# Attention in one table of steps per pair of heads, with one ring of seven PSUM banks

## The chip, the cores and the metric

One core of a Trainium2 chip. TensorE (PE) multiplies and transposes into PSUM (8 banks); ScalarE (ACT), VectorE (DVE) and GpSimd (POOL) work on tiles; SyncE (SP) issues the DMAs from one queue, in order. The metric is the device time of one execution in microseconds (us).

## The reference

Three stages on 896 tokens (2 batches of 448), 12 heads of 64:

```python
# 1: causal attention, q, k, v of shape (2, 12, 448, 64)
scores = np.where(mask, -1e9, (1 / np.sqrt(64)) * (q @ k.T))
attn = np.exp(scores - max); attn = attn / (sum + 1e-9)
x = (attn @ v) as (896, 768)
# 2: h = x @ w_in (768 x 2048); g = 0 below -1, h above 1, (h + 1)**2 / 4 between; x = g @ w_out
# 3: xn = x / rms(x) * rms_g; g = xn @ w_gate; x = (silu(g) * (xn @ w_val)) @ w_out  (768 x 1536)
```

## The kernel before

The program is recorded as a list of operations (`Plan.op`), each with the engines it may run on and a planned length. `Plan.run` puts them in time by their dependences and emits them per engine in the order of the planned starts. Operations recorded through `seq` keep their recorded order on their engine (a chain); the others fill the places between them.

The attention works on pairs of heads: 12 pairs g, each with three units of score chunks: unit 0 is row chunk 3 (448 columns), unit 1 row chunks 2 and 0 (336 and 112 columns), unit 2 row chunk 1 (224 columns). In this document the steps have short names, a digit for the unit and a second one for the head j:

- S (`scores`, L763): the scores of both heads of a unit into two PSUM banks.
- M (`maxima`, L771, DVE): adds the mask and takes the row maximum, in place in the bank.
- E (`exps`, L780, ACT): exponential out of the bank into SBUF (`pn`), with the row sum; after it the bank is free.
- T (`transposes`, L799): TensorE transposes the exponentials into one or two banks. V (`evac`, L823 on ACT, L825 on DVE): copies them to SBUF (`pts`); of the five copies of a pair one is on DVE.
- PV (`pv`, L852): the product with the values into bank 7.
- F (`factor`, L831, L833 on DVE): reciprocals of the sums, then DMAs on SP to DRAM (L835) and back as a broadcast `rb` (L838, two halves).
- X (`xsplit`, L862, DVE): multiplies PV's bank by `rb` into x; after it `operand` makes the operands of the next stage (a cast and a subtraction for each, L298 and L304, often a subtraction ahead).

S takes banks from a ring of four (`sring`), T from a ring of three (`tring`), each in fixed turns; PV has bank 7. The loop over n = 3 g + u records scores(n + 1), maxima(n), exponentials(n), transposes(n - 1), the copies of unit n - 2, and PV of pair g - 1 at u = 2. q is multiplied by 1/8 after it is loaded (`scale_q`, L743: pair 0 on DVE, the others on POOL).

Between these steps the weights of in1 (`w_in`) are loaded and prepared: `w_float` (L346 on ACT, L349 and L359 on DVE) makes fp32 of 64-bit words in blocks of 128 x 768, `split` makes a rounded part (`copy_op`, a cast on ACT, L298) and a remainder (`tt_op`, DVE or POOL, L304). Four such blocks are prepared by the end of the attention.

The next stage, in1 (L491), is made of units of 9 matmuls of 448 columns, one unit for each product of a group of weights (seven products per group; the first unit is product 1 of group 0). It starts once the last PV is through. Then come `plain` (L1026), the second matrix pair (L491 again) and `outer` (L561).

Of the kernel before, what the change touches and what calls it, by code (L numbers as in the profile page):

```python
# [10 lines left out]
F32 = mybir.dt.float32  # L11
# [207 lines left out]
def kernel(  # L219
# [65 lines left out]

    def bank_take():
        i = min(bfree, key=lambda i: bfree[i])
        del bfree[i]
        return i
# [7 lines left out]
    def copy_op(dst, src, n, r, w, **kw):  # L297
        op({"ACT": act_t(n)}, lambda e: nc.scalar.copy(dst, src), r, w, **kw)  # L298
# [29 lines left out]
    def w_float(st, ps, wf):  # L328
# [11 lines left out]
        def words(w, dtype):  # L340
            return ap(st, dtype).rearrange("p (n t) -> p n t", t=2)[:, :, w]

        top = ("top", st.off, len(plan.alts))
        low = ("low", st.off, len(plan.alts))
        op({"ACT": act_t(n)},
           lambda e: nc.scalar.activation(words(1, F32), words(1, F32), ACTF.Prelu, scale=2.0 ** -112,  # L346
                                          alpha=-2.0 ** 32), [st], [top])
        op({"DVE": (dve2_t(n), True)},
           lambda e: nc.vector.tensor_scalar(out=words(0, I32), in0=words(0, I32), scalar1=29, scalar2=0,  # L349
                                             op0=ALU.logical_shift_right, op1=ALU.bitwise_or), [st], [low])  # L350

        def comb(e):
            out, hi, lo = words(1, I32), words(1, I32), words(0, I32)
            if ps:
                out = pst[:, 6:8, :HW].bitcast(I32)
                hi, lo = (x.rearrange("p (h n) -> p h n", h=2) for x in (hi, lo))
            else:
                out = ap(wf, I32)
            nc.vector.scalar_tensor_tensor(out=out, in0=hi, scalar=3, in1=lo, op0=ALU.logical_shift_left,  # L359
                                           op1=ALU.bitwise_or)  # L360
        op({"DVE": (dve_t(n), True)}, comb, [top, low], [st] + ([bk(6), bk(7)] if ps else [wf]))
# [342 lines left out]
    mask = SF.alloc(S)  # L704
    held = qraw + kraw + vraw + [pn] + pts + rbs + [mask]
# [630 lines left out]
```

## Time and profile before

| | us |
|---|---|
| runs: median of 3 (lowest to highest) | 573.09 (568.79 to 574.65) |
| the profiled execution | 571.67 |
| its span | 570.0 |

| engine | busy us | share of the span |
|---|---|---|
| PE | 552.1 | 97% |
| DVE | 476.5 | 84% |
| ACT | 377.5 | 66% |
| POOL | 89.5 | 16% |

The first 102.8 us are the attention, then follows in1 until 206.3. A busy share is an average over stages, and a matmul that has begun and waits inside its group still counts as busy; so the rows below follow the chain of work that ended last and the timeline of single rounds.

### The profile page before, as it was taken

Reading aid. Unit: us, or ns where it says so; the run is one execution under the profiler, and the core shown is the slowest. Engines: PE = TensorE matmul, PEld = TensorE weight load, DVE = VectorE, ACT = ScalarE, POOL = GpSimd, SP = SyncE. Lnnn points to the kernel's source line nnn. Section 1 sums busy time; section 2 is a strip of 40 time slices with the busy share of each in tenths; the row PEclk is TensorE's granted clock in tenths of the full one; section 3 lists DMA queues with packets and bytes.
Section 4 is the critical chain, followed back from the end, with each engine's and each line's share of the span. In section 5 each row is a group of like instructions: output and inputs, shape, how many; then the busy total and the mean of one; then the engine's idle time right before and its main releaser. Section 6 shows DMA issues by size and latency. Waiting matters only on the chain.

```text
span 570.0 us, 8284 instructions
## 1 busy us (share of the span) xinstructions
PE 552.1 (97%) x2890; PEld 475.1 (83%) x2890; DVE 476.5 (84%) x932; ACT 377.5 (66%) x807; POOL 89.5 (16%) x86
## 2 busy tenths in 40 slices
PE   6999998999999999999999988999999999999997
PEld 4555655899998899998999877999989999999896
DVE  4898667999989889844983599999899998999993
ACT  5899888768877888636542553377565748756751
POOL 2323143101002010000000111253301010101400
PEclk9999999999999999999999978999999999999999
DMA  8644633142145468413030310163542434341012
GB/s 257 180 142 137 179 98 67 59 164 99 67 167 160 145 209 281 149 55 110 3 112 0 112 54 0 53 227 111 173 160 112 135 142 163 120 162 48 1 48 97
DMA packets 21496, 67.80 MB, mean 119 GB/s; under 512 B 5264, under 2 KB 11408, under 8 KB 21456
## 3 DMA queue, kind: packets, MB, share of 16 engines
q1 hardware_dynamic: 21456, 67.30, 35.9%
q8 instruction: 22, 0.36, 0.3%
q14 instruction: 18, 0.15, 0.1%
HBM read 64.49 MB, written 2.80 MB: 118 GB/s over the span
## 4 chain that ended last, share of the span: by engine, by line
PE 86%; DVE 6%; DMA 3%; ACT 3%; issue 1%; POOL 0%; SPq 0%; DVEq 0%; ACTq 0%
PE ps L491 38%; PE ps L1026 20%; PE ps L561 13%; PE ps L763 7%; PE ps L799 4%; PE ps L852 4%; DVE sf L304 2%; DMA sf<-in_w_in 1%; DVE sr L304 1%; DMA sf<-in_w_gate 1%; ACT sr L298 1%; DVE sf L359 1%; DVE sf L349 1%; DMA sf<-in_qT 0%; DVE ps L359 0%
## 5 line engine op out<-in xcount | busy, mean ns | idle before, releaser
L491 PE MATMUL ps<-sr 128*128 128x448 f32 x1260 | 262.2, 370 | 1.8 <-ACT sr L298 1.1
L491 PEld LDWEIGHTS ps<-sr 128*128 128x128 f32 x1260 | 239.0, 190 | 24.7 <-ACT sr L298 1.9
L298 ACT CAST sr<-sf 128x384 fp32r<-128x384 f32 (+2 forms) x260 | 137.4, 557 | 81.7 <-DVE sf L304 28.0
L304 DVE TENSOR_TENSOR sr<-sf,sr 128x448 fp32r<-128x448 f32 (+2 forms) x218 | 131.5, 628 | 23.4 <-ACT sr L298 19.0
L1026 PE MATMUL ps<-sr 128*128 128x448 f32 x576 | 118.6, 367 | 0.0
L1026 PEld LDWEIGHTS ps<-sr 128*128 128x128 f32 x576 | 108.2, 188 | 10.1 <-issue 0.4
L304 POOL TENSOR_TENSOR sr<-sf,sr 128x384 fp32r<-128x384 f32 (+2 forms) x42 | 53.0, 1267 | 304.8 <-ACT sr L298 298.0
L304 DVE TENSOR_TENSOR sf<-ps,sf 128x448 f32<-128x448 f32 (+1 forms) x113 | 66.4, 597 | 14.5 <-PE ps L491 7.8
L561 PE MATMUL ps<-sr 128*128 128x448 f32 x378 | 77.1, 366 | 0.0
L561 PEld LDWEIGHTS ps<-sr 128*128 128x128 f32 x378 | 70.8, 188 | 6.2 <-ACT ps L298 0.4
L304 DVE TENSOR_TENSOR sf<-sf 128x448 f32<-128x448 f32 (+1 forms) x88 | 56.0, 663 | 19.0 <-ACT sf L964 18.7
L346 ACT ACTIVATE sf<-sf 128x768 f32<-128x768 f32 x68 | 62.0, 922 | 8.0 <-DMA sf<-in_w_in 2.4
L771 DVE CUSTOM_DVE_ANT_0 ps<-ps,sf 112x336 f32<-112x336 f32 (+2 forms) x96 | 41.8, 465 | 17.5 <-PE ps L763 16.5
L780 ACT ACTIVATE sf<-ps,sf 112x336 f32<-112x336 f32 (+2 forms) x96 | 47.3, 509 | 6.9 <-DVE sf L771 6.0
L359 DVE SCALAR_TENSOR_TENSOR sf<-sf 128x768 int32<-128x768 int32 x50 | 48.3, 975 | 1.4 <-ACT sf L346 0.4
L763 PE MATMUL ps<-sf 64*112 64x448 f32 (+3 forms) x192 | 42.5, 447 | 6.9 <-DVE sf L743 4.5
L304 POOL TENSOR_TENSOR sf<-sf 128x448 f32<-128x448 f32 (+1 forms) x24 | 29.2, 1226 | 88.1 <-DVE sf L304 52.5
L349 DVE TENSOR_SCALAR sf<-sf 128x768 int32<-128x768 int32 x68 | 41.0, 609 | 2.3 <-DMA sf<-in_w_in 0.9
L298 ACT CAST sr<-ps 128x384 fp32r<-128x384 f32 (+1 forms) x54 | 25.4, 489 | 20.0 <-DVE ps L304 8.3
L763 PEld LDWEIGHTS ps<-sf 64*112 64x112 f32 x192 | 18.3, 180 | 22.4 <-ACT sf L780 6.7
L304 DVE TENSOR_TENSOR sr<-ps,sr 128x384 fp32r<-128x384 f32 (+1 forms) x54 | 30.1, 560 | 3.9 <-ACT sr L298 3.1
L298 ACT COPY ps<-ps 128x448 f32<-128x448 f32 x36 | 18.7, 521 | 18.3 <-PE ps L491 17.0
(45 smaller groups left out, 346.2 us busy)
## 6 DMA issues: line engine op xcount, KB each, us to landing
sf<-in_w_out SPq DMA_DIRECT2D x28, 768.0 KB, 4.3
sf<-in_w_in SPq DMA_DIRECT2D x16, 768.0 KB, 4.3
sf<-in_w_gate SPq DMA_DIRECT2D x12, 768.0 KB, 4.3
sf<-in_w_val SPq DMA_DIRECT2D x12, 768.0 KB, 4.5
sf<-in_kT SPq DMA_DIRECT2D x12, 224.0 KB, 3.2
sf<-in_qT SPq DMA_DIRECT2D x12, 224.0 KB, 4.4
sf<-in_v SPq DMA_DIRECT2D x12, 224.0 KB, 3.3
sf<-row SPq DMA_DIRECT2D x24, 112.0 KB, 2.9
```

The lines of the kernel that those rows point to most:

```text
L298: op({"ACT": act_t(n)}, lambda e: nc.scalar.copy(dst, src), r, w, **kw)
L304: op(alts, lambda e: E[e].tensor_tensor(out=dst, in0=a, in1=b, op=alu), r, w, **kw)
L346: lambda e: nc.scalar.activation(words(1, F32), words(1, F32), ACTF.Prelu, scale=2.0 ** -112, alpha=-2.0 ** 32), [st], [top])
L349: lambda e: nc.vector.tensor_scalar(out=words(0, I32), in0=words(0, I32), scalar1=29, scalar2=0, op0=ALU.logical_shift_right, op1=ALU.bitw ...
L359: nc.vector.scalar_tensor_tensor(out=out, in0=hi, scalar=3, in1=lo, op0=ALU.logical_shift_left, op1=ALU.bitwise_or)
L491: nc.tensor.matmul(bank(o), lhsT=ap(d.sub(x * HW + k * P, P)), rhs=ap(t.sub(y * S, S)), start=(begin and k == 0 and i == 0), stop=(k == HK ...
L561: nc.tensor.matmul(bank(o), lhsT=ap(a.sub(x * HW + d * P, P)), rhs=ap(t.sub(y * S, S)), start=(p == 1 and i0 == 0 and i == 0), stop=(i0 == ...
L763: nc.tensor.matmul(pst[:C, bs[j], o:o + (c + 1) * C], lhsT=ap(q)[r, c * C:(c + 1) * C], rhs=ap(k)[r, :(c + 1) * C], start=True, stop=True, ...
L771: seq("DVE", 0.19 + 0.00105 * (c + 1) * C + 0.14, lambda t=t, c=c: nc.vector.tensor_tensor_reduce(out=t, in0=t, in1=ap(mask)[:C, S - (c + ...
L780: seq("ACT", 0.2 + 0.0008 * w + 0.2, lambda c=c, o=o, w=w: nc.scalar.activation(Pn[:C, j, poff[c]:poff[c] + w], pst[:C, sbank[n][j], o:o + ...
L799: nc.tensor.transpose(pst[:C, bs[j][0], o:o + C], Pn[:C, j, poff[c] + kc * C:poff[c] + (kc + 1) * C], ap(ident)[:C, :C])
L1026: nc.tensor.matmul(bank(o), lhsT=ap(w.sub(x * NK * P + d * P, P)), rhs=ap(t.sub(y * S, S)), start=(i0 == 0 and i == 0), stop=(i0 == NM - 1 ...
```

## The change

- **Order.** The loop over n is replaced by a table, `PIPE`, that is walked once per pair: each entry is a step, its unit, its head or half, and a shift of the pair (0, -1 or -2). The recorded order of TensorE's work in a round is S0(g), PV(g-2), T2(g-1), T1(g-1), S2(g), S1(g), T0(g). ACT's is E10, E11, V01, V00 of pair g-1, E01 of g, V20 of g-1, E00 of g, V11 of g-1, E20, E21 of g; V10 is DVE's.
- **Banks.** One ring of seven for S and T: a step takes the bank that was given back the longest ago (`bank_take`), and E or V gives it back. PV keeps bank 7. Bank 6 is reserved from pair NG on.
- **1/8.** `scale_q` is gone; the maximum multiplies by -1/8 instead of -1.
- **Operand casts.** While `early` holds (until the walk reaches pair NG), a cast from SBUF may go to POOL, and `w_float` works in two halves of 384 columns.
- **in1's first unit** is recorded between the last T and the last PV (`run_unit`).
- Ten tiles for x are set aside (`xslots`), and some planned lengths are changed.

TensorE's instructions for one round in the middle of the attention, before (112x448: S0; 64x...: PV; 112x112: T; 112x336, 112x112 x2 and 112x224 of L763: S1 and S2):

```order
L763 MATMUL ps<-sf 112x448 x2
L852 MATMUL ps<-sf 64x336 x2
L852 MATMUL ps<-sf 64x112 x2
L852 MATMUL ps<-sf 64x336 x2
L852 MATMUL ps<-sf 64x224 x2
L852 MATMUL ps<-sf 64x112 x2
L799 MATMUL ps<-sf 112x112 x8
L763 MATMUL ps<-sf 112x336 x2
L763 MATMUL ps<-sf 112x112 x2
L799 MATMUL ps<-sf 112x112 x4
L763 MATMUL ps<-sf 112x224 x2
L799 MATMUL ps<-sf 112x112 x8
```

and of the change:

```order
L765 MATMUL ps<-sf 112x448 x2
L856 MATMUL ps<-sf 64x336 x2
L856 MATMUL ps<-sf 64x112 x2
L856 MATMUL ps<-sf 64x336 x2
L856 MATMUL ps<-sf 64x224 x2
L856 MATMUL ps<-sf 64x112 x2
L802 MATMUL ps<-sf 112x112 x12
L765 MATMUL ps<-sf 112x224 x2
L765 MATMUL ps<-sf 112x336 x2
L765 MATMUL ps<-sf 112x112 x2
L802 MATMUL ps<-sf 112x112 x8
```

The instructions are the same; T1 has moved from the end of the round to behind PV, next to T2, and stands for the pair before, and S1 stands last among the scores.

TensorE from the last PV but one to in1, before (L491: in1):

```order
L852 MATMUL ps<-sf 64x112 x2
L799 MATMUL ps<-sf 112x112 x12
L852 MATMUL ps<-sf 64x336 x2
L852 MATMUL ps<-sf 64x112 x2
L852 MATMUL ps<-sf 64x336 x2
L852 MATMUL ps<-sf 64x224 x2
L852 MATMUL ps<-sf 64x112 x2
L491 MATMUL ps<-sr 128x448 x504
```

and of the change (L504: in1):

```order
L856 MATMUL ps<-sf 64x112 x2
L802 MATMUL ps<-sf 112x112 x12
L504 MATMUL ps<-sr 128x448 x9
L856 MATMUL ps<-sf 64x336 x2
L856 MATMUL ps<-sf 64x112 x2
L856 MATMUL ps<-sf 64x336 x2
L856 MATMUL ps<-sf 64x224 x2
L856 MATMUL ps<-sf 64x112 x2
L504 MATMUL ps<-sr 128x448 x495
```

Nine of in1's matmuls, its first unit, now stand ahead of the last PV.

POOL in the later half of the attention, before (L743: the scaling of q; L304: subtractions and additions):

```order
L743 TENSOR_SCALAR sf<-sf 128x448
L304 TENSOR_TENSOR sr<-sf,sr 128x448
L304 TENSOR_TENSOR sr<-sf,sr 128x384
L743 TENSOR_SCALAR sf<-sf 128x448
L304 TENSOR_TENSOR sr<-sf,sr 128x448
L743 TENSOR_SCALAR sf<-sf 128x448
L304 TENSOR_TENSOR sr<-sf,sr 128x448
L304 TENSOR_TENSOR sf<-sf 128x448
```

and of the change (L305: casts; L311: subtractions and additions):

```order
L305 CAST sr<-sf 128x448
L311 TENSOR_TENSOR sr<-sf,sr 128x448
L311 TENSOR_TENSOR sf<-sf 128x384
L305 CAST sr<-sf 128x384
L311 TENSOR_TENSOR sf<-sf 128x448
L305 CAST sr<-sf 128x448
L311 TENSOR_TENSOR sr<-sf,sr 128x448
L305 CAST sr<-sf 128x384
```

The scalings are gone, and the casts that were ACT's have come.

The diff, cut to its core:

```diff
+    reserved = set()
     def bank_take():
-        i = min(bfree, key=lambda i: bfree[i])
+        i = min((i for i in bfree if i not in reserved), key=lambda i: bfree[i])
...
-    def copy_op(dst, src, n, r, w, **kw):
-        op({"ACT": act_t(n)}, lambda e: nc.scalar.copy(dst, src), r, w, **kw)
+    early = [True]
+    def copy_op(dst, src, n, r, w, ps=True, **kw):
+        alts = {"ACT": act_t(n)}
+        if not ps and early[0]:
+            alts["POOL"] = pool_t(n)
+        op(alts, lambda e: nc.scalar.copy(dst, src) if e == "ACT" else nc.gpsimd.tensor_copy(dst, src), r, w, **kw)
...
+        parts = 2 if early[0] and not ps else 1
+        m = n // parts
+        for i in range(parts):
...
+    xslots = [SF.alloc(S) for _ in range(10)]
...
-    def scale_q(g, eng):
-        if g < NG:
-            q = qraw[g % NQ]
-            seq(eng, 0.6, lambda: E[eng].tensor_scalar(out=ap(q), in0=ap(q), scalar1=float(D) ** -0.5, scalar2=1.0,
-                                                       op0=ALU.mult, op1=ALU.mult), [q], [q])
-    sring, tring = [0, 1, 2, 3], [4, 5, 6]
-    def turn(ring):
-        ring.append(ring.pop(0))
-        return ring[-1]
...
-        sbank[n] = bs = [turn(sring), turn(sring)]
+        sbank[n] = bs = [bank_take(), bank_take()]
...
-                out=t, in0=t, in1=ap(mask)[:C, S - (c + 1) * C:], scale=-1.0, scalar=3e38,
+                out=t, in0=t, in1=ap(mask)[:C, S - (c + 1) * C:], scale=-float(D) ** -0.5, scalar=3e38,
...
+        bank_give(sbank[n][j])
...
-            tbank[n] = [(turn(tring), 0), (turn(tring), 0)]
+            tbank[n] = [(bank_take(), 0), (bank_take(), 0)]
...
+        bank_give(t)
...
+    PIPE = (
+        ("S", 0, 0), ("M", 1, 1, -1), ("E", 1, 0, -1), ("PV", -2), ("E", 1, 1, -1), ("M", 0, 1, 0), ("V", 0, 1, -1),
...
+    VEC = {(1, 0)}
...
+    bfree.pop(7)
...
+    for g in range(NG + 2):
+        if g == NG:
+            reserved.add(6)
+            early[0] = False
+        for what in PIPE:
+            if 0 <= g + what[-1] < NG:
+                if g == NG + 1 and what[0] == "PV":
+                    run_unit()
+                step(what[:-1], g + what[-1])
+        if g < NG:
+            emit_preps(min(2 * g - 16, -3), -1)
```

## Rows read from the trace of the kernel before

**Rows 1.** Windows: stretch; us, then each engine's busy us; TensorE clock, DMA share, GB/s.

```profile
23.98:87.12 63.14, 61.71 (x448) 36.75 (x448) 49.65 (x173) 56.02 (x181) 22.01 (x25) 1.00 0.52 146
...
102.81:206.30 103.49, 103.34 (x507) 94.59 (x506) 94.61 (x163) 82.47 (x154) 14.79 (x11) 1.00 0.38 128
```

**Rows 2.** Chain that ended last, 38 to 50 us: start, us, engine and line.

```profile
40.08 1.82 PE ps L763 x4
41.90 2.04 PE ps L852 x20
43.94 0.91 PE ps L799 x8
44.85 0.95 PE ps L763 x8
45.79 0.53 PE ps L799 x4
46.32 0.57 PE ps L763 x4
46.89 0.91 PE ps L799 x8
```

**Rows 3.** Timeline, same round: start, us, engine, line, operation; [idle before <-releaser].

```profile
40.89 0.27 PEld L763 LDWEIGHTS ps<-sf 64*112 64x112 f32 x2 [0.57 <-ACT sf L780]
...
45.83 0.52 DVE L771 CUSTOM_DVE_ANT_0 ps<-ps,sf 112x336 f32<-112x336 f32 x1 [0.24 <-PE ps L763]
...
46.87 0.54 ACT L780 ACTIVATE sf<-ps,sf 112x336 f32<-112x336 f32 x1
...
47.47 0.95 DVE L862 TENSOR_TENSOR sf<-ps,sf 128x448 f32<-128x448 f32 x1
...
47.73 0.54 ACT L780 ACTIVATE sf<-ps,sf 112x336 f32<-112x336 f32 x1
```

**Rows 4.** Chain that ended last, 0 to 25 us.

```profile
4.02 0.41 DVE sf L743
...
4.46 1.89 PE ps L763 x4
...
16.22 1.81 PE ps L763 x4
```

**Rows 5.** Chain that ended last, 84 to 110 us.

```profile
87.21 1.81 PE ps L763 x4
...
100.77 2.11 PE ps L852 x20
```

**Rows 6.** Timeline of SP's DMA issues; then the broadcast's line, issue to landing.

```profile
28.36 0.42 SPq L835 DMA_DIRECT2D row<-sf  x1
34.43 1.09 SPq L838 DMA_DIRECT2D sf<-row  x2
...
44.40 0.38 SPq L835 DMA_DIRECT2D row<-sf  x1
47.96 1.09 SPq L838 DMA_DIRECT2D sf<-row  x2
...
DMA to landing us min/median/max: 2.7/2.9/5.4
```

**Rows 7.** Groups by form on ACT and POOL, 23.98 to 87.12: busy us, mean ns.

```profile
L298 ACT CAST sr<-sf 128x384 fp32r<-128x384 f32 x9 | 4.8, 532 | 0.6 <-POOL sf L304 0.6
L298 ACT CAST sr<-sf 128x448 fp32r<-128x448 f32 x8 | 4.6, 580 | 0.0
...
L743 POOL TENSOR_SCALAR sf<-sf 128x448 f32<-128x448 f32 x7 | 4.1, 582 | 34.6 <-DMA sf<-in_qT 24.4 <-DVE sf L771 7.0 <-PE ps L799 3.2
```

**Rows 8.** Timeline, POOL beside DVE; then the line L831: min/median/max ns.

```profile
42.64 1.00 POOL L304 TENSOR_TENSOR sf<-sf 128x384 f32<-128x384 f32 x1
...
42.80 0.87 DVE L831 TENSOR_SCALAR sf<-sf 112x8 f32<-112x8 f32 x1
...
L831 DVE TENSOR_SCALAR sf<-sf x12: 154/160/867, 12.3 to 99.2; 112x8 f32<-112x8 f32 x12
```

More of the change, by code (lines that the diff above doesn't have):

```diff
@@ L308, in split @@
         x, k = (ap(src), src) if ps is None else (ps[0], ps[1])
-        copy_op(ap(hi), x, n, [k], [hi])
+        copy_op(ap(hi), x, n, [k], [hi], ps=ps is not None)
         tt_op(ap(lo), x, ap(hi, F32), ALU.subtract, n, [k, hi], [lo], ps=ps is not None)
@@ L338, in w_float @@
             return wf
[L340 to L361, printed above, removed]
+        parts = 2 if early[0] and not ps else 1
@@ L802, in transposes @@
         r = [pn_k(j, c) for j in range(2) for c, _ in UNITS[u]]
-        seq("PE", (0.97, 0.97, 0.6)[u], fn, r, sorted({bk(x[0]) for x in bs}), tail=0.1)
+        seq("PE", (0.88, 0.88, 0.48)[u], fn, r, sorted({bk(x[0]) for x in bs}), tail=0.1)
         if u == 2:
@@ L825, in fn @@
                 nc.vector.tensor_copy(out, src)
-        seq(eng, 0.5 if eng == "ACT" else 0.58, fn, [bk(t)], w)
+        seq(eng, 0.5 if eng == "ACT" else 0.56, fn, [bk(t)], w)
+        bank_give(t)
     def factor(g):
@@ L1185 @@
     load_qk(2)
-    scale_q(0, "DVE")
-    scale_q(1, "POOL")
     preps.sort(key=lambda x: (x[0], x[2], x[1]))
@@ new lines, with step @@
+    PIPE = (
[4 rows of a table added]
+    )
+    VEC = {(1, 0)}
+    def step(what, g):
+        kind, *a = what
+        n = g * NU + a[0] if a else g
+        if kind == "S":
+            scores(n)
+            if a[0] == 1:
+                load_qk(g + 3)
+        elif kind == "M":
+            maxima(n, a[1])
+        elif kind == "E":
+            exps(n, a[1])
+        elif kind == "T":
+            transposes(n)
+        elif kind == "V":
+            evac(n, a[1], "DVE" if (a[0], a[1]) in VEC else "ACT")
+        elif kind == "PV":
+            pv(g)
+            load_v(g + 2)
+        elif kind == "F":
+            factor(g)
+        else:
+            xsplit(g)
@@ new lines, with run_unit @@
+    bfree.pop(7)
+    nu = 0
+    def run_unit():
+        nonlocal nu
+        now[0] = nu
+        while later and later[0][0] <= nu:
+            later.pop(0)[1]()
+        emit_preps(nu, nu)
+        units[nu]()
+        nu += 1
+    for g in range(NG + 2):
[9 more added lines that the diff above has]
+            emit_preps(min(2 * g - 16, -3), -1)
@@ L1279 @@
     staged[1] = 3
-    for i in range(6):
-        bank_give(i)
-    for i, f in enumerate(units):
-        now[0] = i
-        while later and later[0][0] <= i:
-            later.pop(0)[1]()
-        emit_preps(i, i)
-        f()
+    del bfree[6]
+    while nu < len(units):
+        run_unit()
     body = tc.manual_schedule()
```

94 lines of the change are left out of this document (30 added, 64 removed), and 3 rows, old and new, of the table PIPE.

## The prediction

> **What bounds the kernel now.** I read the busy time by stretch first [rows 1]. From 102.81 to 206.30, in1, TensorE is busy 103.34 of 103.49 us: nothing can be gained there but by starting earlier. The attention ahead of it is the part with slack that is hard to see: TensorE is "busy" 61.71 of 63.14 us in its steady part, but a matmul that waits for a bank in the middle of its group counts as busy. So I read the chain of work next [rows 2], for one round (one pair of heads). It is all TensorE, and one piece stands out: the scores of unit 0 (448 columns, x4) take 1.82 us, where the scores of unit 1, as many columns (336 + 112), take 0.95. The timeline says why [rows 3]: the weight load for the second head's half of S0 sat idle 0.57 us until ACT's exponentials (L780) let go of a bank. S0 of pair g+1 gets, from the ring of four, the two banks of unit 1 of pair g, whose exponentials are the longest chain in the round and follow the maxima that start only at 45.83. The useful TensorE work of a round is the sum of the six other pieces of [rows 2], 2.04 + 0.91 + 0.95 + 0.53 + 0.57 + 0.91 = 5.91, and 0.95 for an unhindered S0: 6.86 us. What a round takes: S0 of pair 2 starts at 16.22 and S0 of pair 11 at 87.21 [rows 4, 5], 9 rounds in 70.99, so 7.89 each. About 1.03 us per round is wait.
>
> The rest of the loss is the drain: the last PV runs only from 100.77, for 2.11 us [rows 5], so from S0(11) at 87.21 to the first product of in1 at 102.88 pass 15.67 us. The gaps in it are waits of PV and of in1 for copies on ACT, which stand behind operand casts there.
>
> **The change, part by part.**
>
> *Order of a round, TensorE.* The instructions are the same, in the order S0(g), PV(g-2), T2(g-1), T1(g-1), S2(g), S1(g), T0(g). With the pieces above they end at 0.95, 2.99, 3.52, 4.43, 5.00, 5.95 and 6.86 us of the round. Three chains through the other engines must fit.
> (a) S1, M1, E1, T1. S1 ends at 5.95. The two heads' M1 take 1.64 us (45.83 to 47.47, [rows 3]), so they end at 7.7; E1 of a head takes 0.86 (46.87 to 47.73, [rows 3]), and the second cannot start before the second M1 is done, so both end near 8.7, which is 1.85 of the next round. T1 wants them at 3.52: some 1.6 us to spare, where the old order had less than none.
> (b) Banks. When S0 of the next round is issued, S1 and T0 hold four; S2's two exponentials are through by then (S2 ends at 5.00, its maxima and exponentials need about 1.4); so three of seven are free and S0 takes two. At S1 (5.00) S2 holds two and the tail of T1 at most two, so S1 gets its two. I find no step at which an issue must wait, with under 1 us of margin at S1.
> (c) The row of reciprocals. X(g-1) needs rb, which goes SBUF to DRAM to SBUF on SP's queue. On that queue the row's issue stands behind the load of V, which waits for PV. PV(g-2) ends at 2.99, the row is issued at about 3.5; to the broadcast's issue passed 3.56 us at 44.40 and 6.07 at 28.36, where a weight load was issued just ahead; the second half of the broadcast is issued 0.55 later and lands after 2.9 in the median [rows 6]. So rb is there at 3.5 + 3.56 + 0.55 + 2.9 = 10.5, which is 3.65 of the next round, and X could start at 3.1. It is 0.5 late, and 3.1 late with 6.07. DVE works in order, so V10 and M20 queue behind X; but S2 ends at 5.00, so M20 cannot start before 5.1, and X (0.95) with V10 fit until X starts at about 3.6. The common case is at the edge of free; the bad one eats the 1.6 us of chain (a), plus about 1 us, in the at most three rounds that have a weight load ahead. I take 0.3 us in all for (c), between 0 and 3.
>
> *Demand of the other engines per round* (the first window of [rows 1] holds 8 rounds). ACT: 56.02/8 = 7.0, more than 6.86, so it would now be the bound if nothing left it. The casts go to POOL: 9 of 532 ns and 8 of 580 [rows 7], 9.4 us or 1.18 per round; 5.8 stay. The weight blocks prepared in the loop are four before and after. DVE: 49.65/8 = 6.2 at most, less what subtractions go to POOL. POOL: the new program issues 21 casts and 30 two-operand subtractions or additions up to in1, 15 of 384 columns, 1.00 us each [rows 8], and 15 of 448, 1.17 by their length: 33 us. A cast on POOL is in no row: its floor is nothing, its nearest row the one-input TENSOR_SCALAR of 448 columns (582 ns, [rows 7]), its ceiling the two-input 1.17. I take 0.57, since it reads one input too: 12 us, so 45 us over 12 rounds, 3.7 of 6.86; with the ceiling 58 us, 4.8. No engine reaches 6.86.
>
> *The shared port.* At 42.80 the 8-column TENSOR_SCALAR of F took 0.87 us, against 0.16 in the median of 12, while a POOL operation ran from 42.64 to 43.64 [rows 8]. So DVE's short SBUF operations wait out a POOL operation. POOL's share grows from 22.01/63.14 = 35% [rows 1] to 3.7/6.86 = 54%. F and about 1.5 pieces of weight per round are exposed: 2.5 x 0.54 x half of 1.0 = 0.7 us per round, of which 35/54 was in the 6.2 already. DVE ends near 6.4: no bound, little room. The Trainium skill, "SBUF — State Buffer", section "Who interferes with whom", says that DVE and GpSimd share one port pair as an exclusive lock, held for the whole instruction, so the loser does not slow down but stops; it speaks against moving casts to POOL. The trace agrees in this row (0.87 for 0.16). Taken at its worst it gives the slower case below.
>
> *1/8 in the maximum.* The scale moves into a constant that the instruction has anyway. It removes eleven POOL operations of 0.58 and one on DVE at the start: 0.41 us at 4.02, right ahead of the first matmul at 4.46 [rows 4], on the path. The first two rounds otherwise hold the same matmuls, waiting on new chains; from 4.46 to 16.22 took 11.76. I put S0(2) at 16.0, a gain of 0.2 (bounds: 15.0 if they never wait, and 16.6).
>
> *Half-size weight pieces and fixed X slots* cost two more ACT and DVE operations per block; both lie under TensorE (ACT 5.8 of 6.86). If that cover went, four blocks at three extra starts of about 0.1 would be 1.2 us.
>
> *Drain.* After S0(11), 87.21 before: round 11 (6.86), PV(10) 2.04, T2 and T1 1.44, in1's first product, then PV(11) 2.04. The product is work taken from in1 (9 of its 504 matmuls), so it counts as nothing, and its 1.8 us cover the copies after T1(11), three on ACT or DVE in about 1.1. So 12.4 instead of 15.67: a gain of 3.3.
>
> *Sum.* Loop: 9 rounds x (7.89 - 6.86) = 9.3, less 0.3 for (c): 9.0. Drain 3.3, start 0.2: 12.5. in1 keeps its length if its operands keep up. DVE was busy 94.61 of 103.49 us there, 91% [rows 1], and X(11) with the operands made from it falls into in1's first products in both programs. I take 0.5 back, bounds 0 and 1.5. Gain 12.0. The profiled execution took 571.67 us, span 570.0 and 1.67 around it, so 559.7; the median of the three runs is 573.09, 1.42 higher, and they spread from 568.79 to 574.65. I forecast 560.0.
>
> **The rivals.**
> 1. *rb late in every round.* If the row needs 6.07 us each time [rows 6], X starts at 6.2 of the round, T1 is about 0.6 late, and a round takes 7.45: loop 9 x 0.44 = 4, drain 2.7, so 565. For it: SP's order, and (c) has no room. Against: 6.07 was seen with a weight load in front.
> 2. *The wait only moves.* If S0's wait comes back at another bank of the one ring, the round stays near 7.9 and only the drain gains: 568.5. For it: seven banks before and after. Against: chain (a).
> 3. *in1 takes half back.* If the pieces of weight that lie in the loop, about 0.6 us per round and 7 in all, slid behind it, DVE would have 101.6 us of work in in1, and at the 91% that it reached there this takes 111, 8 us more than now. For it: DVE is the busiest engine beside TensorE there. Against: the same four blocks are ready at in1's start in both, and POOL takes some of DVE's subtractions. Between 0 and 8 back, so 564.
> 4. *Slower.* Each of the 2.5 exposed DVE operations waits out a whole POOL operation of 1.17: 2.9 per round instead of 0.7, DVE 8.6. It decides from a wait of 2.2 us per round, where DVE passes 7.89. At 8.6 the loop loses 9 x 0.7 = 6.4, the drain gains 3.3 - 1.7 = 1.6, and the first two rounds, without X some 7.6 each instead of 5.9, lose 3.4: 580. For it: the row on the lock. Against: 0.16 is the median of 12, with POOL busy 35%.
>
> **How the numbers follow.** Forecast (556.5 to 562.5): 0.68. Rival 1: 0.10, rival 2: 0.08, rival 3: 0.08, rival 4: 0.05; 0.01 for better still. A measurement of this kernel tells about 1% (5.7 us) from no change. The forecast, rival 3, most of rival 1 and the last make 0.85 faster; rival 2 and the rest of 1 make 0.10 the same; 0.05 slower. The range from 554 to 567 takes in the spread of the runs (3 us to either side) and rivals 1 and 3; it leaves out 2 and 4.
>
> **What would show it.** Right: in the chain of the changed kernel S0 takes 0.95 in the loop, rounds take 6.8 to 7.0 us, no weight load of L765 waits for ACT, in1's remaining products start near 92, with 1.8 us of product between T1(11) and PV(11); POOL casts near 0.57. Wrong: X (now L866) idle for DMA from the row in most rounds (rival 1); TensorE idle or a stretched S0 in the loop (rival 2); pieces of DVE or ACT in the chain between 100 and 190 with TensorE idle (rival 3); F and the weight pieces on DVE at 0.9 or more each (rival 4).

## The result and the profile after

The changed kernel is slower, by 0.8%. 20 runs of each in turn gave a median of 574.21 us (571.93 to 579.65) against 570.38 (566.59 to 575.84), a ratio of 1.0084 with a 95% interval of 1.0058 to 1.0110. The forecast was 560.0, with a range from 554 to 567. By the prediction's own classes, which begin at 1%, this is no change, to which it gave 0.10; but the interval leaves 1 out. The profiled execution of the change took 573.64 us, its span 571.9 (before: 571.67 and 570.0).

The table follows three places through both programs: the scores of unit 0 of the third and the last pair, S0(2) and S0(11); the start of in1's tenth product, with which everything but the first unit is still to come; and the end of the span. "Forecast" puts the terms of the prediction on the same scale, with in1's tenth product at 1.9 behind its first. Starts are read to 0.1 us.

| us | before | forecast | after |
|---|---|---|---|
| S0(2) | 16.2 | 16.0 | 14.8 |
| S0(11) | 87.2 | 78.0 | 84.6 |
| in1's tenth product | 104.8 | 92.3 | 100.5 |
| from there to the end | 465.2 | 465.7 | 471.4 |
| span | 570.0 | 558.0 | 571.9 |

Of the 12.5 us that the attention should give, it gave 4.3; and the stages behind it, which the prediction left alone, took 6.2 more.

*Where the attention lost it.* Five of the nine rounds are near the forecast of 6.86: the one from 50.2 takes 6.65, and from S0(7) at 56.8 to S0(11) at 84.6 four take 6.95 each. The first, from 14.8, takes 7.7; DVE waited 2.1 us for a weight load until 15.3. And three rounds, from 22.6 to 50.2, take 27.6. SP's DMA issues there:

```profile
25.33 0.75 SPq L842 DMA_DIRECT2D sf<-row  x1
26.18 0.53 SPq L747 DMA_DIRECT2D sf<-in_kT  x1
26.75 0.43 SPq L750 DMA_DIRECT2D sf<-in_qT  x1
27.22 0.43 SPq L329 DMA_DIRECT2D sf<-in_w_in  x1
27.75 0.38 SPq L741 DMA_DIRECT2D sf<-in_v  x1
28.23 0.37 SPq L839 DMA_DIRECT2D row<-sf  x1
35.23 1.09 SPq L842 DMA_DIRECT2D sf<-row  x2
```

The second half of a broadcast is late, so the loads queued behind it on SP come in one bunch (3 x 224 KB and 768 KB of weights), and then the row of reciprocals, 3.5 KB. The chain that ended last (start, us, what) shows what that does:

```profile
28.23 6.99 DMA row<-sf
...
35.74 2.90 DMA sf<-row
...
39.62 0.63 DVE sf L828
...
40.29 1.00 PE ps L802 x4
41.29 1.77 PE ps L765 x4
43.06 3.65 PE ps L856 x20
46.70 1.29 PE ps L802 x12
```

The row lands after 6.99 us. X on DVE (L866) waits 4.27 us for the broadcast and the copy V10 (L828) stands behind X; T1 waits for V10, and TensorE stands still for 3.17 us (timeline):

```profile
38.76 0.94 DVE L866 TENSOR_TENSOR sf<-ps,sf 128x448 f32<-128x448 f32 x1 [4.27 <-DMA sf<-row]
...
40.29 1.00 PE L802 MATMUL ps<-sf 112*112 112x112 f32 x4 [3.17 <-DVE sf L828]
41.22 1.84 PE L765 MATMUL ps<-sf 64*112 64x448 f32 x4
```

When it goes on, the granted clock has dropped (windows: stretch; us; busy us of PE, PEld, DVE, ACT, POOL; clock, DMA share, GB/s):

```profile
37.20:40.29 3.09, 0.00 (x0) 0.00 (x1) 1.53 (x3) 0.00 (x0) 0.53 (x1) 0.86 0.78 228
40.29:43.06 2.77, 2.77 (x10) 1.16 (x12) 2.27 (x12) 2.43 (x10) 1.17 (x2) 0.50 0.19 50
43.06:46.70 3.64, 3.64 (x21) 1.98 (x22) 1.97 (x7) 2.17 (x8) 1.50 (x2) 0.56 0.89 236
46.70:50.20 3.50, 3.50 (x36) 2.87 (x34) 3.29 (x10) 2.70 (x9) 2.33 (x3) 1.00 0.71 238
```

0.50 is the lower level, 1.2 GHz: after 3 us without a matmul S0 takes 1.84 and PV 3.65 instead of 0.94 and 2.04. The three rounds together take 7.0 us more than 3 x 6.86: 3.2 are the standstill, 2.5 the half clock, and the rest lies in pieces that wait a little before it, S0 among them (1.30 and 1.34).

*The drain* has the same wait in it. The chain, and X(10) in DVE's timeline:

```profile
84.67 0.94 PE ps L765 x4
...
94.51 1.87 PE ps L504 x9
96.38 2.04 issue
98.42 2.11 PE ps L856 x20
100.53 1.62 PE ps L504 x7
```

```profile
96.84 0.94 DVE L866 TENSOR_TENSOR sf<-ps,sf 128x448 f32<-128x448 f32 x1 [2.99 <-DMA sf<-row]
...
97.70 0.62 DVE L828 COPY sf<-ps 112x448 f32<-112x448 f32 x1
```

in1's first unit does lie between T1(11) and PV(11), but then TensorE stands for 2.04 us. X(10) waits for its row, which was late too; PV(11) needs bank 7, which X(10) gives back at 97.78, and the copy V10(11) (L828), which stands behind X(10) on DVE and ends at 98.32. PV(11) starts 0.10 after the copy, so the copy is what ends the wait.

*The later stages.* in1 from its tenth product on and `plain` are 1.0 and 1.2 us shorter than before; the second matrix pair, with the normalisation at its start, is 4.1 longer, and the last stage, `outer`, 4.4 longer. In `outer` DVE's share is as high as before, and it is busy 4 us longer (the first window is the change, the second before):

```profile
487.00:570.00 83.00, 80.19 (x379) 70.04 (x377) 74.26 (x132) 44.74 (x90) 10.43 (x6) 1.00 0.22 78
```

```profile
489.50:567.50 78.00, 76.88 (x378) 70.38 (x377) 70.22 (x128) 43.22 (x88) 8.57 (x4) 1.00 0.22 81
```

and the change's chain there runs over weight loads and DVE:

```profile
485.55 4.61 DMA sf<-in_w_out
...
494.10 6.12 DMA sf<-in_w_out
...
500.25 0.57 DVE sf L360
```

where before all of it was TensorE:

```profile
489.47 76.70 PE ps L561 x377
```

The planner has put DVE's later operations, the same ones, in another order: about 4 of 5 agree with before.

### The profile page after: what moved, and what is told of

Same layout as the page of the kernel before. It is cut to its first block, busy times and chain, and to the rows that moved or that the text cites. A ratio compares the mean times of both kernels' runs of the same rounds, so it can differ in the third digit from the quotient of the medians.

```text
span 571.9 us, 8276 instructions
## 1 busy us (share of the span) xinstructions
PE 548.8 (96%) x2890; PEld 474.8 (83%) x2890; DVE 473.3 (83%) x922; ACT 368.6 (64%) x790; POOL 113.4 (20%) x113
## 4 chain that ended last, share of the span: by engine, by line
PE 77%; DVE 14%; DMA 4%; issue 2%; ACT 1%; SPq 0%; DVEq 0%; ACTq 0%
PE ps L504 36%; PE ps L1030 20%; PE ps L574 7%; DVE sf L311 6%; PE ps L765 5%; DVE sr L311 5%; PE ps L802 4%; PE ps L856 4%; DMA sf<-in_w_out 2%; DVE sf L371 1%; DMA row<-sf 1%; DVE sf L360 1%; ACT sr L305 1%; DMA sf<-row 1%; DMA sf<-in_qT 0%
## 5 line engine op out<-in xcount | busy, mean ns | idle before, releaser
L504 PE MATMUL ps<-sr 128*128 128x448 f32 x1260 | 261.5, 368 | 2.6 <-ACT sr L305 1.1
L504 PEld LDWEIGHTS ps<-sr 128*128 128x128 f32 x1260 | 236.5, 188 | 27.0 <-DVE sf L311 2.0
L305 ACT CAST sr<-sf 128x384 fp32r<-128x384 f32 (+2 forms) x239 | 126.9, 557 | 92.8 <-DVE sf L311 35.0
L311 DVE TENSOR_TENSOR sr<-sf,sr 128x448 fp32r<-128x448 f32 (+2 forms) x202 | 126.4, 655 | 27.3 <-ACT sr L305 23.5
L311 POOL TENSOR_TENSOR sr<-sf,sr 128x384 fp32r<-128x384 f32 (+1 forms) x58 | 70.2, 1218 | 290.2 <-ACT sr L305 267.7
L311 DVE TENSOR_TENSOR sf<-ps,sf 128x448 f32<-128x448 f32 (+1 forms) x113 | 66.5, 597 | 15.5 <-PE ps L504 9.3
L311 DVE TENSOR_TENSOR sf<-sf 128x448 f32<-128x448 f32 (+1 forms) x87 | 53.9, 646 | 17.0 <-ACT sf L968 16.4
L357 ACT ACTIVATE sf<-sf 128x768 f32<-128x768 f32 (+1 forms) x72 | 62.7, 879 | 5.4 <-DMA sf<-in_w_out 1.9
L782 ACT ACTIVATE sf<-ps,sf 112x336 f32<-112x336 f32 (+2 forms) x96 | 47.5, 505 | 17.0 <-DVE sf L773 16.7
L371 DVE SCALAR_TENSOR_TENSOR sf<-sf 128x768 int32<-128x768 int32 (+1 forms) x54 | 49.9, 928 | 1.3 <-ACT sf L357 0.4
L311 POOL TENSOR_TENSOR sf<-sf 128x448 f32<-128x448 f32 (+1 forms) x25 | 31.2, 1251 | 94.8 <-DVE sf L311 77.3
L360 DVE TENSOR_SCALAR sf<-sf 128x768 int32<-128x768 int32 (+1 forms) x72 | 41.5, 585 | 2.8 <-DMA sf<-in_w_in 2.1
L305 ACT CAST sr<-ps 128x384 fp32r<-128x384 f32 (+1 forms) x54 | 25.7, 491 | 23.8 <-DVE ps L311 9.0
L765 PE MATMUL ps<-sf 64*112 64x448 f32 (+3 forms) x192 | 36.4, 453 | 4.1 <-DMA sf<-in_qT 4.1
L311 DVE TENSOR_TENSOR sr<-ps,sr 128x384 fp32r<-128x384 f32 (+1 forms) x54 | 30.1, 560 | 4.7 <-ACT sr L305 4.2
L802 PE MATMUL ps<-sf 112*112 112x112 f32 x240 | 29.7, 268 | 3.3 <-DVE sf L828 3.2
L856 PEld LDWEIGHTS ps<-sf 112*64 112x64 f32 x240 | 16.0, 143 | 18.3 <-issue 9.7
```

The source lines that it names most:

```text
L305: op(alts, lambda e: nc.scalar.copy(dst, src) if e == "ACT" else nc.gpsimd.tensor_copy(dst, src), r, w, **kw)
L311: op(alts, lambda e: E[e].tensor_tensor(out=dst, in0=a, in1=b, op=alu), r, w, **kw)
L357: lambda e, words=words: nc.scalar.activation(words(1, F32), words(1, F32), ACTF.Prelu, scale=2.0 ** -112, alpha=-2.0 ** 32), [part], [top])
L360: lambda e, words=words: nc.vector.tensor_scalar(out=words(0, I32), in0=words(0, I32), scalar1=29, scalar2=0, op0=ALU.logical_shift_right, ...
L504: nc.tensor.matmul(bank(o), lhsT=ap(d.sub(x * HW + k * P, P)), rhs=ap(t.sub(y * S, S)), start=(begin and k == 0 and i == 0), stop=(k == HK ...
L765: nc.tensor.matmul(pst[:C, bs[j], o:o + (c + 1) * C], lhsT=ap(q)[r, c * C:(c + 1) * C], rhs=ap(k)[r, :(c + 1) * C], start=True, stop=True, ...
```

## The experiments

Names: **a_** is an edit of the changed kernel, **b_** of the kernel before. "Tenth product" is in1's, its start in the profiled execution; "rest" is from there to the end of the span. A profiled execution can lie up to 4.5 us from its kernel's median (a_nn: 578.1 for 573.61). So verdicts on a few us go by the ratios, to the kernel before on the same chip; the profiles show the mechanism. No ratio here is further than 2% from 1.

| kernel | S0(11) | tenth | rest | ratio [95%] |
|---|---|---|---|---|
| before | 87.2 | 104.8 | 465.2 | 1 |
| after | 84.6 | 100.5 | 471.4 | 1.0084 [1.0058, 1.0110] |
| a_norb | 81.1 | 94.8 | 470.7 | 0.9950 [0.9919, 0.9982] |
| a_actq | 86.6 | 100.7 | 474.2 | 1.0086 [1.0046, 1.0126] |
| a_rowfirst | 81.2 | 96.6 | 470.7 | 0.9963 [0.9929, 0.9996] |
| a_both | 83.9 | 98.1 | 473.0 | 0.9959 [0.9916, 1.0001] |
| a_late | 75.8 | 108.3 | 473.5 | one run, 583.51 us |
| b_castpool8 | 91.9 | 109.4 | 466.1 | 1.0052 [1.0008, 1.0096] |
| b_fill | 87.6 | 103.2 | 474.8 | 1.0108 [1.0050, 1.0167] |
| a_noslots | 84.3 | 100.2 | 479.6 | 1.0147 [1.0088, 1.0206] |
| a_nofill | 85.9 | 104.3 | 475.1 | 1.0171 [1.0097, 1.0246] |
| a_nn | 89.5 | 109.8 | 466.2 | 1.0049 [1.0012, 1.0085] |
| a_rf_nn | 81.2 | 100.0 | 464.9 | 0.9947 [0.9921, 0.9974] |
| a_rf_nn_xl | 85.5 | 105.1 | 465.5 | 0.9969 [0.9935, 1.0002] |
| a_rf_nn_xl_ch | 85.3 | 103.9 | 464.4 | 0.9976 [0.9943, 1.0009] |
| a_t8 | 88.9 | 103.1 | 471.2 | 1.0083 [1.0047, 1.0119] |
| a_rf_nn_xl_t8 | 83.4 | 103.0 | 465.0 | 0.9905 [0.9872, 0.9937] |
| a_rf_nn_xl_t8_ca | 82.7 | 98.0 | 465.2 | 0.9888 [0.9845, 0.9930] |
| b_eighth | 100.1 | 117.6 | 461.2 | 1.0152 [1.0114, 1.0190] |
| a_best_h | 83.2 | 99.5 | 466.5 | 0.9921 [0.9893, 0.9948] |

### The wait for the row

**a_norb**: only the first two pairs fetch their reciprocals; the kernel leaves out the normalisation of the others.

```diff
+            if g < 2:
                 seq("SP", ... dma_start(out=row ..., in_=rs[:C]) ...)   # and the broadcast
-            [bk(xb), ("rb", g % 2, 0), ("rb", g % 2, 1), rb], [x])
+            [bk(xb), rb], [x])
```

> The change, but only the first two pairs fetch their reciprocals; the ten others multiply with what lies there (their own normalisation is left out), so no X waits for a DMA in the loop. Theory R (the row of reciprocals): the attention's missing 8 us are X's waits for it, with the stall of TensorE and the half clock that follows; then no two rounds take 18.6 us as between 22.62 and 41.22, every round takes 6.9 to 7.1, and in1's products behind the last PV start at 93 to 94.5 instead of 100.53. Theory B (banks and the shared port): they start at 98 or later. If the stages behind in1 keep their length, R gives 567 and B 573; if they are planned anew with another length, the starts in the trace still tell R from B.

From the fifth pair on rounds take 6.5 us, and the tenth product comes 5.7 earlier (94.8, just past the expected 93 to 94.5), though one stall is left, among the two pairs that still fetch: there DVE waits for a weight load that took 7.14 us. The seven rounds from S0(4) to S0(11), with weight loads and the work on weights still in them, take 45.6 us; in the change they take 54.1. So the row's way costs those rounds 8.5 us, most of what the attention missed.

**a_actq**: the attention's weight loads are issued by ACT instead of SP. **a_rowfirst**: V's load is recorded behind F instead of behind PV, so the row goes first on SP. **a_both**: the two together.

```diff
             pv(g)
-            load_v(g + 2)                            # a_rowfirst
...
             factor(g)
+            if g > 0:
+                load_v(g + 1)
...
-            op({"SP": 0.1}, ... nc.sync.dma_start(out=ap(st, I32), ...   # a_actq
+            op({"ACT": 0.1}, ... nc.scalar.dma_start(out=ap(st, I32), ...
```

> The change, with the weight loads of the attention issued on ACT's queue instead of SP's. If the row was slow because it stood in one queue behind a load of 768 KB, it lands in at most 3.5 us, the stall is gone, and in1's products start at 94 to 96 (time 568 to 569). If the load slows it through the shared DMA engines, the row still takes 6 to 7 us beside a load and they start near 100 (574).

> The change, with the row of reciprocals ahead of the load of V on SP's queue, so that it no longer waits for PV: it is issued about 1.1 us earlier in the round. Theory R: the common rounds lose their small X waits, the bad one shrinks by 1 to 2 us, in1's products start at 97.5 to 99 (571 to 572). Theory B: no change, 100.5 and 574.

> The row ahead of V, and the weight loads on ACT's queue. Theory R: no X waits, in1's products start at 93 to 95, near the run without reciprocals, 567 to 569. Theory B: 99 or later.

Another queue for the weights does not help: with two weight loads under way from ACT's queue, the row at 18.44 took 6.88 us and a broadcast 8.91, and X waits 11.0 us in four rounds; rows issued just ahead of a load took 3.1 and 3.4. So SP's order is not the whole of it; here a load under way delayed the small transfers though it came from another queue (without such loads, in a_late below, the row took 4.2 at most). The row ahead of V's load helps, 4 us and a ratio of 0.9963. Both together are no better than that.

**a_late**: the weight loads are held back to the attention's end.

```diff
-               tail=4.6, rel=rel)
+               tail=4.6, rel=84.0 if early[0] else rel)
```

> The changed kernel with its weight loads of the attention held back to the attention's end (not before 84 us of planned time); nothing else is changed. Theory 'weight loads': without them the row lands after 2.2 to 3 us each time, X waits under 2 us for it in all up to the last pair (10.7 in the change), ACT and DVE never wait for in_w_in, rounds take 6.5 to 7.0 throughout, so the scores of the last pair start at 74 to 78 (84.6 in the change, 87.2 before). in1 then waits for its first weights, so the tenth product is late (105 to 115) and the time 580 to 595. Rival 'the row by itself' (SP's order and the path over DRAM are too slow for the table even without loads): X waits 6 us or more, last pair at 82 or later.

The span of attention without a weight load in it (windows as above), and the row's issue to landing there:

```profile
14.50:75.80 61.30, 60.56 (x505) 40.75 (x504) 48.32 (x178) 51.34 (x177) 16.88 (x19) 1.00 0.47 129
```

```profile
DMA to landing us min/median/max: 1.9/3.1/4.2
```

Nine rounds in 61.3, and the clock at 1.00 throughout; in the change they took 69.8, and its row landed after 2.2/3.3/7.0. The order of steps does what it promised; with the weight loads in, the nine rounds are 8.5 us longer. a_late takes the work on the weights out of these rounds as well, so alone it does not tell the loads from that work; a_norb, which keeps both and drops the row, does. One expectation missed: X still waits 5.5 us for the row, in four rounds. The table absorbs about half of that: rounds without a wait take 6.51, and nine of them 58.6. The loads themselves are needed, as the tenth product at 108.3 shows.

### The order of the later work

Each of these changes the recorded program ahead of in1 and looks at the rest. **b_castpool8**: casts on POOL and 1/8 in the maximum, on the kernel before; VectorE's later order stays that of before. **b_fill**: in1's first unit ahead of the last PV, alone. **a_noslots**, **a_nofill**, **a_nn**: the change without the tiles for x, without the early first unit, without either; only the last has before's later order.

```diff
-    xslots = [SF.alloc(S) for _ in range(10)]
+    xslots = []                                  # a_noslots, a_nn
-                if g == NG + 1 and what[0] == "PV":
-                    run_unit()                   # a_nofill, a_nn
             if g == NG:
+                bank_give(0)
+                run_unit()                       # b_fill
                 pv(g - 1)
```

b_castpool8 takes the lines of the change's diff on `copy_op`, `scale_q` and the scale of the maximum.

> The kernel before with two parts of the change alone: casts may go to POOL while the attention runs, and 1/8 stands in the maximum; order of steps, banks, in1's first unit and tiles for x stay as before. Theory 'order of later work' (the later stages are longer in the change because in1's first unit and the tiles set aside for x give the planner another order of VectorE's later operations): here that order is the one of before, row for row, so the normalisation takes 19.2 us (+-0.6) and the last stage 76.7 (+-1.0). Theory 'earlier means later' (the later stages are longer whenever in1 starts earlier): it depends on the start, which here is 100 to 104 us against 104.8, and the last stage would be 77 to 81. On the attention: with the casts off ScalarE the wait of S0 shrinks, in1's later products start 1 to 4 us earlier than 104.8 (the theory that POOL's casts cost nothing); 105 or later by the theory that VectorE's waits for POOL cost what ScalarE gains. Whole: 567.5 to 570.5, or 571 to 574 by the rivals.

> The kernel before with in1's first unit recorded ahead of the last PV, and nothing else of the change. Attention: the 1.8 us of that unit now cover the copies that the last PV waits for; in1's later products start at 102.5 to 103.5 instead of 104.8, or at 104.8 if the last PV then waits for its bank (X of the pair before), as in the change. Theory 'order of later work': VectorE's later order is neither that of before nor that of the change (it agrees with either in about 80 of 100 operations), and the later stages are off by more than 1 us from before's 19.2 and 76.7 if the first unit's place is the cause, within 1 us if the tiles for x are. Whole: 569 if the later stages keep their length, 572 to 575 if not.

> The changed kernel with the ten tiles for x not set aside (the allocator places each x, as before). VectorE's later order is then neither the one of before nor the one of the change. Attention as in the change (later products of in1 from 99 to 102). Theory 'order of later work', with the tiles as its cause: the last stage comes back to 76.7 (+-1.0) and the normalisation to 19.2, so 567 to 569. With the first unit as the cause: 80 to 82 and 21 to 21.6 as in the change, so 573 to 575. Theory 'earlier means later': 80 to 82 too.

> The changed kernel with in1's first unit behind the last PV, as before. Attention: the last PV is still held by its bank until about 98.4, the first unit follows it, so in1's later products start near 102.4 instead of 100.5 (the theory that the drain is bound by the wait for X of the pair before); if the wait goes with the unit, 100.5. Theory 'order of later work', with the first unit as its cause: last stage 76.7 (+-1.0), normalisation 19.2, so 569 to 571; with the tiles for x as the cause 80 to 82 and 21 to 21.6, so 575 to 577.

> The changed kernel without two of its parts at once: the tiles for x are not set aside, and in1's first unit stands behind the last PV. VectorE's later order is then the one of before, row for row. Theory 'order of later work': from in1's tenth product to the end 465 to 466.5 us, as in the two kernels with that order (before 465.2; before with casts on POOL 466.1), against 471.4 in the change and 474.8 to 479.6 with one of the two parts alone. The tenth product at 104 (+-1), as without the first unit alone, so the span 569 to 571 and the time 570.5 to 572.5, as before. Theory 'earlier means later': 470 or more from there to the end, so 576 or more.

The column "rest" sorts itself. All kernels with before's later order have 461 to 466.5, whether in1 starts at 98 or at 117.6; all others have 470.7 to 479.6. So the rest goes with the order, not with the earlier start. The traces bear the grouping out: from the second matrix pair on, DVE, ACT and POOL take their operations in before's order in the first group and in another in the second. The three orders change together, so the runs do not tell whose counts. Nor does the order fix the exact length: b_fill and a_noslots have the same one there and are 4.8 us apart. Neither the first unit nor the tiles alone makes the difference: each of the two taken out alone makes the rest longer still (479.6 and 475.1). The set-aside tiles win back some of what the early first unit does to the order. That this is so, and not why one order is worth 9 us more than another, is what the runs show.

a_nn's tenth product missed its expectation (109.8 for 104): three stalls like the one above, from 22.9 to 61.9. b_castpool8's came 4.6 later than before's, which its rival (105 or later) had; but ACT and DVE wait 4.9 us for weight loads there, up to 95 us, where before it was 0.4, and its order of steps is the old one, so this is no matter of the new table. That led to the weight loads' own lateness.

### Late weight loads

**a_rf_nn** is a_nn with the row first. **a_rf_nn_xl** also moves X behind M2; **a_rf_nn_xl_ch** also puts the weight loads into SP's recorded order.

```diff
-               tail=4.6, rel=rel)
+               tail=4.6, rel=rel, chain="SP" if early[0] else None)   # a_rf_nn_xl_ch
-... ("E", 0, 1, 0), ("X", -2), ("T", 1, -1),
+... ("E", 0, 1, 0), ("T", 1, -1),
-        ("M", 2, 1, 0), ("T", 0, 0),
+        ("M", 2, 1, 0), ("X", -2), ("T", 0, 0),
```

> As the kernel with neither part (later order of before), and the row of reciprocals is issued ahead of V's load. Theory 'wait for rb': in1's tenth product 4 us earlier than without, as it was with the first unit in (96.6 against 100.5): 98.5 to 100.5. With 465 to 466.5 to the end: span 564 to 567, time 565.5 to 568.5. If what the two theories give doesn't add (the later stages wait for weights when in1 begins earlier): 570 to 572.

> As the one before it (row ahead of V's load, later order of before), and X stands behind the maxima of S2 in the table, not ahead of V10. Theory 'wait for rb': a late row may be 2 us later without holding V10 and the maxima behind X on VectorE; the two rounds of 8.2 and 8.6 us in the kernel with the row first (44.1 to 60.9) fall to 7, so the tenth product comes 2 to 3.5 us earlier, at 95.5 to 98, and the time is 562 to 565.5. Rival: X ahead of M1 delays it by its 0.95 us, chain (a) has no room for it, rounds take 7.3 or more everywhere, and the time is 567 or more.

> As the one before it, and the weight loads of the attention are issued in recorded order, at the end of a round behind the loads of q and k. If the place of a load beside the row still matters: tenth product 0.5 to 2 us earlier than in that kernel and the idle of X for the row under 1 us in all. If X's later place already covers the late rows: the same within 0.5 us. If SP, which works in order, now waits with the load for a free buffer while the row stands behind it: 1 to 4 us later. Later stages 465 to 466.5 in each case.

a_rf_nn came as expected and is faster than before, by 0.5%. a_rf_nn_xl missed, by 7 us (105.1 for 95.5 to 98); a_rf_nn_xl_ch came 1.2 earlier than that, as expected (0.5 to 2), but their ratios do not tell them apart, or from 1. The later X did end its waits for the row, to nothing, but not the stalls (chain of a_rf_nn_xl):

```profile
36.65 6.70 DMA sf<-in_w_in
...
43.37 0.02 ACT sf L357
...
43.84 1.81 ACT sf L782 x8
45.69 0.72 PE ps L802 x4
```

The planner counts on a weight load after 4.6 us; this one took 6.70. ACT works in order and stands with the first piece of the weights until it lands, with the exponentials behind it. Such waits sum to 6.9 us on ACT (9.0 in a_rf_nn_xl_ch). So a load that lands late can delay the row, and it can block ACT or DVE directly.

**a_t8**: the change, with 8 us of planned landing (`tail`) for the attention's weight loads. **a_rf_nn_xl_t8**: the same on a_rf_nn_xl. **a_rf_nn_xl_t8_ca**: casts back on ACT as well. **b_eighth**: before, with 1/8 in the maximum alone. **a_best_h**: a_rf_nn_xl with casts on ACT and the first four loads as halves of 384 KB, one per round, planned to land after 6.

```diff
-               tail=4.6, rel=rel)
+               tail=8.0 if early[0] else 4.6, rel=rel)               # ..._t8
-        if not ps and early[0]:
-            alts["POOL"] = pool_t(n)                                  # ..._ca, a_best_h
-    scale_q(0, "DVE")
-    scale_q(1, "POOL")
-            scale_q(g + 2, "POOL")
-                ... scale=-1.0, scalar=3e38,
+                ... scale=-float(D) ** -0.5, scalar=3e38,             # b_eighth
+    half_at = [4.0, 8.0, 14.0, 21.0, 28.0, 35.0, 42.0, 49.0]
+                for i in range(2):
+                    op({"SP": 0.1}, ... [st.sub(i * h, h)], tail=6.0, rel=half_at.pop(0))   # a_best_h
```

> As the kernel with the row first, the later order of before and X behind the maxima of S2; in addition the planner is told that a weight load of the attention lands 8 us after its issue, not 4.6 (6 to 7 measured). Theory 'late weights': ACT and DVE, which work in order, no longer stand behind a piece of weight whose load is under way; their waits for in_w_in up to 95 us fall from 10.5 us to under 2, rounds take 6.6 to 7.0 from the fourth pair on, in1's tenth product comes at 96 to 98.5 (105.1 without), later stages 464.5 to 466.5, time 562.5 to 566. Rival 'the wait only moves': X waits 5 us or more for the row again, or the copies wait for a free buffer; tenth product 101 or later, time 567 to 571.

> The changed kernel with the planned landing of the attention's weight loads alone at 8 us in place of 4.6. Theory 'late weights': ACT's and DVE's 3.5 us of waits for in_w_in go, but X still waits 9 to 11 us for the row, which the loads delay: tenth product 98 to 100.5, later stages 471 as in the change, time 571 to 574. Rival 'the row alone': nothing moves, 100.5 and 574. If the loads are issued so differently that the row no longer meets them: 95 to 97, time 568 to 570.

> As the first of these, with the operand casts of the attention left on ACT as before. Theory 'the casts had to go': ACT has 7.0 us of work per round instead of 5.8 and is the bound of a round of 6.6 to 6.9, so rounds take 7.1 to 7.5 and the tenth product comes 2.5 to 6 us later. Rival 'POOL's lock costs what ACT gains': the short operations of F take 0.16 to 0.31 instead of 0.95, and the tenth product comes within 1 us of the first or earlier. Later stages 464.5 to 466.5.

> The kernel before with 1/8 in the maximum and no scaling of q. From the working: 0.4 us at the start, and POOL free of eleven operations off the path: tenth product 104.2 to 104.8, later order of before, time 570 to 572. If it is this part that brought the stalls of the kernel with both parts (casts on POOL too), because q is needed no longer by POOL and the loads behind it on SP come earlier: 107 to 109.5, time 573.5 to 576.

> As the kernel with the row first, later order of before, X behind the maxima of S2, planned landing longer and casts on ACT (tenth product at 98.0), but each of the first four weight loads is issued as two halves of 384 KB, one per round behind the loads of q and k. Theory 'weight loads': the row has half as many bytes in front of it, lands after 4 us or less, X waits under 3 us in all (6.3 without), rounds 6.6 to 7.1, tenth product 94.5 to 97, time 562 to 565. Rival: the halves stand in front of eight rows instead of four, X waits as long as before in all, tenth product 97.5 to 100, time 565.5 to 568.

With the honest landing time ACT and DVE no longer wait for weights in a_rf_nn_xl_t8, and X waits 6.8 us for the row again: the rival's wait that moves, in part. The tenth product missed its 96 to 98.5 by 4.5 us, but by the ratios it is the clearest gain so far, 0.9905. a_t8 missed too, at 577.31, and shows that the planned landing is not enough by itself: X waits 16.7 us. The late X has a price too: it gives bank 7 back late, and in a_rf_nn_xl_t8_ca TensorE's PV waits 3.7 us for X, in three rounds. Casts on ACT or on POOL make no difference that the intervals can tell (0.9888, 0.9905), and rounds of 6.5 to 6.6 occur with casts on ACT too. The halves ended X's waits (0.2 us), but ACT and DVE wait 12 us for halves that were issued late; the ratio is the same as without.

b_eighth was to be the harmless part and is the worst of all in the attention. Its chain:

```profile
13.55 1.67 PE ps L799 x8
...
72.48 6.63 DMA sf<-in_w_in
...
79.21 0.56 DVE sf L349
...
81.74 2.69 PE ps L763 x3
84.43 3.86 PE ps L852 x20
```

DVE waits for weights 7.2 us in all, 0.4 in the kernel before, where the loads are issued at 21.12, 26.34 and 60.59 instead of 23.74, 29.22 and 72.48. So the kernel before is free of these stalls by where its loads happen to lie, and an edit that moves the plan by a microsecond or two can bring them in: it did in b_eighth and b_castpool8, not in b_fill. S0(2) comes 2.7 us later too: the first matmul starts 0.5 later, and the first two rounds take 2.2 more. The same transposes before:

```profile
11.70 0.91 PE ps L799 x8
```

T at 10.11 and at 13.55 takes 1.67 us, and S0 between them 1.84, as it did at a granted clock of 0.50 above. So these rounds ran at half clock, by the lengths; the windows view shows no lower clock there, but its first clock record is at 16.4, against 8.3 before. Why the clock rose later is open.

The best kernel is a_rf_nn_xl_t8_ca, the new order with the row first, X late, casts on ACT, before's later order and the longer planned landing: 565.84 us (4 runs) against 571.85, 1.1% faster.

## Why the prediction was wrong

- **S0's wait, right in part.** It was to go to nothing. S0 took 1.82 before [rows 2]; in the change it takes 0.94 in two of the nine rounds, 1.30 to 1.34 in five and 1.17 in one; the remaining one ran at half clock. From the chain of the change (start, us, what):

```profile
22.62 1.30 PE ps L765 x4
...
50.23 0.94 PE ps L765 x4
...
56.88 1.34 PE ps L765 x3
```

  The second head's half of S0 still waits for ACT there. In a_norb S0 takes 0.94 in every round from 35.5 on, so with no row to wait for this wait is gone, as the prediction had it.
- **A round of 6.86, right in sum, by luck.** Without weight loads nine rounds took 61.3, where 9 x 6.86 and 0.3 were put at 62.0. The pieces are shorter than taken (6.5 with T2 and T1 together at 1.29 and S2 and S1 at 1.32), and small waits that follow from X's fill that up.
- **(c), the row of reciprocals, failed, and with it the loop.** It was taken at 0.3 us, between 0 and 3; measured are 8.5, the difference to a_norb in the seven rounds from S0(4) on (the difference to a_late, over all nine, is 8.5 too). Against the forecast's 62.0 for nine rounds the loop is 7.8 too long. Three parts of that step were wrong. The row was to be issued at 3.5 of the round; it was issued at 5.6 (28.23 for S0 at 22.6), because the loads behind the previous broadcast on SP were not counted. The worst landing, 6.07, was taken from a round with slack [rows 6]; it was 6.99. And "about 1 us" for what is left of it ignored that TensorE, after its standstill of 3.17 us, came back at half clock. Rival 1 had the mechanism, but at 0.6 in every round; here most of it, 7.0 us, fell into three rounds around one row.
- **The demand of ACT, wrong, with no effect that the runs can tell.** 7.0 us per round was to force the casts to POOL. With casts on ACT and the new order (a_rf_nn_xl_t8_ca) it is busy 56.31 us in nine rounds, 6.3 each.
- **POOL, right.** 21 casts, the larger ones 568 ns and the smaller 502, for the 0.57 taken [rows 7]:

```profile
L305 POOL CAST sr<-sf 128x448 fp32r<-128x448 f32 x11 | 6.2, 568 | 20.4 <-DVE sf L866 20.1
L305 POOL CAST sr<-sf 128x384 fp32r<-128x384 f32 x10 | 5.0, 502 | 19.1 <-DVE sf L371 18.9
L835 DVE TENSOR_SCALAR sf<-sf x12: 162/173/1007, 11.1 to 93.3; 112x8 f32<-112x8 f32 x12
```

  DVE's wait for POOL occurs as in [rows 8], up to 1.007 for 0.173 in F, but seldom: three of the 12 take more than 0.31, each beside a POOL operation. So rival 4 was right that the kernel is slower, and its reason was not.
- **Start, mis-sized.** 0.2 taken, 1.4 measured (S0(2) at 14.8, just outside the bound of 15.0). b_castpool8, without the new table, has S0(2) at 15.2, so most of it is not the table's.
- **Drain, half right.** 3.3 taken. From S0(11) to the tenth product it was 17.6 before and is 15.9, a gain of 1.7. The missing 1.6 is PV(11)'s wait for the copy behind X(10), again the row: in a_norb it is 13.7, a gain of 3.9.
- **in1 and what follows.** That DVE would take 0.5 back in in1 did not show. That the stages behind in1 keep their length was taken without being stated as a step; from in1's tenth product to the end they took 6.2 us more, where 0.5 was put down. The order of DVE's later operations was there to be read in the two programs, and only the places around the edits were read.

## What to carry to other kernels

In a pipeline whose chains have 1 to 2 us to spare, every transfer that shares the DMA engines with large loads is to be costed at its worst landing, and every piece of background work on an in-order engine at its load's measured landing, not at the planned one; here one miss that idled TensorE cost the wait and the half clock after it. Where a planner orders the program, compare the order of all later work before and after, not only of the part edited: kernels that take the same operations in another order were 5 to 14 us longer here. And test an edit that looks free by itself: it moves what the tuned plan had placed well.

## What was not expected of the hardware

TensorE's steady rate differs at one granted clock. In `plain` the kernel before issues 292 matmuls in 60 us, the change 296, both without idle time and at 1.00:

```profile
210.00:270.00 60.00, 60.00 (x292) 54.33 (x290) 42.30 (x60) 37.78 (x56) 0.00 (x0) 1.00 0.45 155
```

```profile
210.00:270.00 60.00, 60.00 (x296) 55.29 (x295) 42.44 (x62) 34.78 (x52) 0.00 (x0) 1.00 0.42 148
```

The count can lack a record or two; the stage's length does not: 118.7 us before and 117.5 in the change. In one profiled execution of each of the 20 kernels the stage takes one of these two, within 0.2. So a difference of 1 us in the column "rest" can come from this alone. Why is open.
